# A two-block fp32 kernel on one core: moving the key decays' transfers, the W_in sums and the W_out negations

## The chip, the cores and the metric

The kernel runs on one core of a Trainium2 chip. The metric is the device time of one execution in microseconds (us). An execution that is profiled gives a page and a trace; "span" is the time from its first to its last instruction, and the execution's own time is a little longer. Engines: TensorE (PE; PEld are its weight loads), VectorE (DVE), ScalarE (ACT), GpSimd (POOL) and SyncE (SP), which only issues transfers.

## What is computed

A recurrent retention block (4 batches, 8 heads, 768 positions, head size 64) and then a two-layer block on its 3072 x 512 output, with 2048 hidden values:

```python
gamma = 1.0 - 2.0 ** (-5.0 - np.arange(H))
for t in range(S):
    state = gamma * state + einsum('bhd,bhe->bhde', k[:, :, t], v[:, :, t])
    y[:, :, t] = scale * einsum('bhd,bhde->bhe', q[:, :, t], state)
x = y.transpose(0, 2, 1, 3).reshape(B * S, H * D)
h = x @ w_in
sp = np.maximum(h, 0.0) + np.log1p(np.exp(-np.abs(h)))
g = h * erf(sp)
out = g @ w_out
```

All of it is float32 on the chip. W_in and W_out come as 64-bit words and are turned into fp32 on the chip.

## The kernel before

**Retention** is done in chunks of 128 positions, j = 0 to 23. The decays are put in by scaling keys and queries with a power of gamma for each position (`kq_s`), and later chunks (j of 6 and more) use a second layout in blocks of 32 positions, whose scales are `kq_b` and `by_b`. `load_block_scales` (L506) fills their first column from the constant key decays: 16 small transfers issued by GpSimd (L510, 0.5 KB each) and one for `by_b` (L514). `block_scales` (L516) makes the rest: three small DVE operations (L517 to L519), then five GpSimd products (L521). `prepared(j)` (L574) scales and transposes a chunk on DVE in five steps.

**The weights** are loaded in 14 pieces by SP (L281, L289) into parts of the weight tiles that are still unused, and converted by DVE and ACT (`whole_conversion`, L302, with L325 to L342; `shifted_conversion`, L349). The first piece of W_in is the first that a matmul needs.

**The two-layer block** works in groups. Groups g = 0 to 3 (the first 512 rows of x, `hidden` and `project`) each make 512 of the 2048 hidden values with plain matmuls (L895, L931). `hidden(g, u)` ends in an ACT copy into `HS[g]` (L913). Groups 4 to 23 (G0 = 4, NG = 24) come in pairs, one pair to a chunk of 256 rows; the even group of a pair uses the first half of the weights (s = 0), the odd one the second (s = 1). They use a fast matrix product: 26 products for the first layer and seven for the second, which need sums of blocks:

- `sum_in(s, upto)` (L381) makes the 30 sums of W_in's half s in place, in the order of the table `W_SUMS`: one DVE operation of 128x256 each (L385). It makes those not yet made, up to the number given.
- `sums(s)` (L388), run through `last_steps`, makes four blocks of W_out's half s: ACT copies a block negated (L393), then GpSimd issues a transfer of 512 KB within SBUF that adds another block to it (L394). The second block, T2, is made from the first, T1, and the fourth, T4, from T2; the third, T3, stands for itself.
- `x_sums(g)` (L956) makes sums of x, `hidden_steps(g)` (L977) the first layer. A step is a product of two weight blocks with one block of x into one of four PSUM banks (L986); the readings of that bank then follow, the first to write a part of h on ACT (L1000, L1002), the others adding to it on DVE (L998). A bank is written again by a later step once it has been read: step 9 writes the bank of step 5, step 15 that of step 13, step 25 that of step 24.
- After the first layer come the softplus (L858, ACT), a visit of the retention (`sub_visit`, L754, with the mask L676), the error function (L865, ACT), and `gated(g)` (L881), two DVE products of 128x1024 (L884). The second layer of group g - 1 (`project_part`, L1069) stands partly inside the first layer of group g, after steps 14, 18 and 24, and partly behind it.

**The order** is written by hand: every engine runs its instructions in the order in which the program names them, and waits on semaphores where it needs another engine's result. In the loop over the groups, tables named `order` say after which of the 26 steps a piece of other work (`next_chunk`, `e_sums`, `w_sums`, `last_steps`) is put in. For groups 0 to 3 the table `after` does this; `load_block_scales` stands there behind the last part of group 2's first layer. Nothing in its transfers waits for that place: GpSimd's queue issues them as soon as it comes to them. `put_first(tt)` (L942) copies a result of the first 512 rows on ACT (L944).

Of the kernel before, what the change touches and what calls it, by code (L numbers as in the profile page):

```python
# [48 lines left out]
W_SUMS = (  # L49
    (16, 2, 6, "+"),  # L50
    (17, 8, 10, "-"),
    (4, 4, 17, "+"),
    (10, 10, 16, "+"),
    (18, 16, 4, "-"),
    (19, 18, 5, "-"),
    (20, 1, 19, "-"),
    (20, 0, 20, "+"),
# [82 lines left out]
def kernel(  # L140
# [13 lines left out]
    nc = tc.nc  # L154
# [9 lines left out]
    N = FG * TCH  # L164
# [58 lines left out]
    idle_out = const.tile([P, 1], F32, name="idle_out")  # L223
# [8 lines left out]
    def w_out_of(ft):  # L232
        half, s, i = ft // (2 * FG), ft % (2 * FG) // FG, ft % FG
        return w_out_sb[:, s, 2 * half : 2 * half + 2, i, :]
# [144 lines left out]
    in_sums = [0, 0]  # L379

    def sum_in(s, upto):  # L381

        assert all(("hidden", 2 * FG + s * FG + u) in done for u in range(FG))
        for to, a, b, sign in W_SUMS[in_sums[s] : upto]:
            nc.vector.tensor_tensor(w_in_sb[:, s, to], w_in_sb[:, s, a], w_in_sb[:, s, b], op=OP[sign])  # L385
        in_sums[s] = max(in_sums[s], upto)
# [25 lines left out]
    def later_sums():  # L412
        for s in range(2):
            yield from sums(s)

    weight_steps = weights()
    last_steps = later_sums()
# [9 lines left out]
    def need(*what):  # L427
        nonlocal room
        while what not in done:
            cost = next(weight_steps, None)  # L430
            if cost is None:
                next(last_steps)
            room -= cost or 0
# [69 lines left out]
    kq_b = const.tile([P, NC, 2, HP, 4], F32, name="kq_b")  # L503
    by_b = const.tile([P, 2, HP], F32, name="by_b")

    def load_block_scales():  # L506
        for s, d in itertools.product(range(2), range(2)):
            part = slice((2 * s + d) * 32, (2 * s + d + 1) * 32)
            for u in range(HP):
                nc.gpsimd.dma_start(  # L510
                    kq_b[part, 0, 0, u],
                    decay_k[:, 2 * u + s : 2 * u + s + 1].rearrange("(a p) h -> p (a h)", p=32),
                )
        nc.gpsimd.dma_start(by_b[:, 1], decay_s)  # L514
# [25 lines left out]
    def ret_psum(pool=None):  # L540

        pool = pool or (next(psum_turn) if early else ps_r)
        return pool.tile([P, HP, C], F32, name="hp" if pool is ps_h else "r")
# [121 lines left out]
    def sub_scores(j):  # L665
        for hp in range(HP):
            for a, s in itertools.product(range(2), range(2)):
                t, own = slice(a * D, (a + 1) * D), slice(s * D, (s + 1) * D)
                nc.tensor.matmul(  # L669
                    SC[j][s][t, hp, :D], KT[j][own, hp, t], QT[j][own, hp, t], start=True, stop=True,  # L670
                )
# [11 lines left out]
    def sub_additions(j):  # L683

        for u in range(HP):
            for r in range(2):
                for a in adds_of[j]:
                    t, h = slice(a * D, (a + 1) * D), 2 * u + r
                    nc.tensor.matmul(
                        SC[j][a][r * D : (r + 1) * D, u, D:], KQ[j][t, 0, h, :], V[j][t, h, :],  # L690
                        start=True, stop=True,
                    )
        pace(1)
# [55 lines left out]
    def sub_begin(j, pool=None):  # L749
        SC[j] = [ret_psum(pool) for _ in range(2)]  # L750
        sub_scores(j)
        sub_additions(j)
# [98 lines left out]
    HS, E, O = {}, {}, {}  # L851

    def gate_softplus(g):


        name = "r" if g < 4 and g % 2 else "e"
        E[g] = act.tile([P, N], F32, name=name, bufs=1)
        nc.scalar.activation(E[g], HS[g], AF.Softplus)  # L858
# [10 lines left out]
    def pace_around(n):  # L869


        pace(n / 2)
        run(waiting)
        waiting.clear()
        pace(n / 2)
# [5 lines left out]
    def gated(g, part=None):  # L881
        for a in range(2) if part is None else (part,):
            half = slice(a * N // 2, (a + 1) * N // 2)
            nc.vector.tensor_tensor(E[g][:, half], HS[g][:, half], E[g][:, half], op=ALU.mult)  # L884
            pace(-1.1)
# [34 lines left out]
    def project(g, tt):  # L920
        if g == 0 and tt == 0:
            O[0] = [ps_o.tile([P, d_model], F32, name=f"o{i}") for i in range(TT)]
        step = tt
        if g:
            of = [(tt, u) for u in range(FG)]
        else:
            of = [(step % 2 * 2 + i // 2, step // 2 * 2 + i % 2) for i in range(4)]
        need("out", g * FG + max(u for _, u in of))
        for tt, u in of:
            ft = g * FG + u  # L930
            nc.tensor.matmul(  # L931
                O[0][tt].rearrange("p (d c) -> p d c", d=2),
                E[g][:, u * TCH + tt * P : u * TCH + (tt + 1) * P],
                w_out_of(ft),
                start=(ft == 0),
                stop=(ft == n_ft - 1),
            )
        if step == TT - 1:
            done.add(("project", g))
        pace_around(3.4)  # L940

    def put_first(tt):  # L942
        o = E[G0 - 1].rearrange("p (u t c) -> p t u c", u=FG, t=TT)[:, tt]
        nc.scalar.copy(o, O[0][tt].rearrange("p (u c) -> p u c", u=FG))  # L944
        nc.sync.dma_start(out[tt * P : (tt + 1) * P, :].rearrange("p (u c) -> p u c", u=FG), o)
# [7 lines left out]
    def chunk_of(g):  # L953
        return TCH // SCH + (g - G0) // 2
# [186 lines left out]
    def next_scores():  # L1141
# [31 lines left out]
            ([], []),  # L1173
            ([], []),
            ([(T, 5)], []),
            ([(load_block_scales,)], []),
        ],
        [
            ([(load, 6), (sub_results, 5)], []),
# [34 lines left out]
    def all_of(steps):  # L1214
        for _ in steps:
            pass
# [10 lines left out]
    load(j + 2)  # L1227
    gated(G0 - 1)
    next(last_steps)
    project(G0 - 1, 0)  # L1230
    put_first(0)
    sum_in(0, len(W_SUMS))
    next_chunk = prepared(j + 1)
    next(next_chunk)
    sub_begin(j)
    sub_states(j)
    next(last_steps)
    project(G0 - 1, 1)
    put_first(1)
    sum_in(1, 8)  # L1240
    order = {8: (last_steps,), 20: (next_chunk, last_steps)}
    order.update({n: (next_chunk,) for n in (10, 14, 16)})
    for n, _ in enumerate(hidden_steps(G0), start=1):
        for steps in order.get(n, ()):
            next(steps, None)
    all_of(next_chunk)
    nc.scalar.activation(idle, idle, AF.Softplus)
    gate_softplus(G0)
    sub_visit(j, G0)
    load(j + 3)  # L1250
    gate_erf(G0)
    sum_in(1, 20)
    for tt in range(2, TT):
        project(G0 - 1, tt)
        put_first(tt)
    gated(G0)
    sum_in(1, 24)
    j += 1

    def sums_left(s):  # L1260
        while in_sums[s] < len(W_SUMS):
            sum_in(s, in_sums[s] + 1)
            yield

    w_sums = sums_left(1)
    put = None
    for g in range(G0 + 1, NG):
        even = (g - G0) % 2 == 0
        more = j < NJ
        if put is not None:  # L1270
            put_part(put, 0)
        e_sums = g_sums(g - 1)
        next(e_sums)
        next_chunk = prepared(j + 1) if even or put is None else iter(())

        if put is not None:
            order = {18: (e_sums,), 20: (e_sums,), 24: (e_sums, e_sums)}
        else:
            order = {
                10: (next_chunk,), 14: (next_chunk, e_sums), 16: (next_chunk, e_sums),  # L1280
                18: (next_chunk, e_sums), 20: (e_sums,), 24: (next_chunk,),
            }
        if g == G0 + 1:
            order.update({n: (w_sums,) for n in (1, 2, 3, 4, 5, 6)})
            order.update({n: (last_steps,) for n in (11, 17, 23)})
        for n, _ in enumerate(hidden_steps(g), start=1):
            if put is not None and n in (14, 16, 18):
                put_part(put, n // 2 - 6)
            for steps in order.get(n, ()):
                next(steps, None)  # L1290
            if n in (14, 18, 24):
                project_part(g - 1, {14: 1, 18: 2, 24: 4}[n])
        put = None
        all_of(e_sums)
        all_of(next_chunk)

        nc.scalar.activation(idle, idle, AF.Softplus)
        gate_softplus(g)
        if more:
            sub_visit(j, g)  # L1300
        all_of(w_sums)
        if g == G0 + 1:
            all_of(last_steps)
        if g + 1 < NG and not even:
            x_sums(g + 1)
        if more:
            if even:
                all_of(prepared(j + 2))
            if j + 3 < NJ:
                load(j + 3)  # L1310
            j += 1
        gate_erf(g)
        for p in (5, 6, 7, 3):
            project_part(g - 1, p)
        if even:
            put = chunk_of(g - 1)
        if g == NG - 1:
            last_gated(g)
        else:
            gated(g)  # L1320

    g, m = NG - 1, chunk_of(NG - 1)
# [68 lines left out]
```

## Time and profile before

| | |
|---|---|
| median of 3 runs | 665.0 us (664.99 to 665.27) |
| the profiled execution, its own time | 664.47 us |
| its span | 662.8 us |
| PE busy in the span | 654.1 us (99%), 6240 instructions |
| DVE busy | 504.5 us (76%) |
| ACT busy | 289.6 us (44%) |
| GpSimd busy | 21.0 us (3%) |
| granted TensorE clock, mean | 1.000 |

The views used below: the page; the waits (for each engine and line, whom it waited for, with the sum, the number of times and the longest in us); the timeline (start in us from the beginning of the span, length in us, engine, line, operation, what it writes and reads, how many in a row, and in brackets the idle time of the engine before it and what ended it); and the windows (the busy time and number of instructions of each engine in a stretch, then granted clock, busy share of the 16 DMA engines and GB/s). Neighbouring matmul records overlap, since matmuls are pipelined.

### The profile page before, as it was taken

Reading aid. Unit: us, or ns where it says so; the run is one execution under the profiler, and the core shown is the slowest. Engines: PE = TensorE matmul, PEld = TensorE weight load, DVE = VectorE, ACT = ScalarE, POOL = GpSimd, SP = SyncE. Lnnn points to the kernel's source line nnn. Section 1 sums busy time; section 2 is a strip of 40 time slices with the busy share of each in tenths; the row PEclk is TensorE's granted clock in tenths of the full one; section 3 lists DMA queues with packets and bytes.
Section 4 is the critical chain, followed back from the end, with each engine's and each line's share of the span. In section 5 each row is a group of like instructions: output and inputs, shape, how many; then the busy total and the mean of one; then the engine's idle time right before and its main releaser. Section 6 shows DMA issues by size and latency. Waiting matters only on the chain.

```text
span 662.8 us, 15378 instructions
## 1 busy us (share of the span) xinstructions
PE 654.1 (99%) x6240; PEld 556.5 (84%) x6240; DVE 504.5 (76%) x1112; ACT 289.6 (44%) x410; POOL 21.0 (3%) x48
## 2 busy tenths in 40 slices
PE   8999999999999999999999999999999999999998
PEld 7744454476999999999999999999999999999997
DVE  5899989978886787778678678777787688476464
ACT  3368594445534344244244243442442542533440
POOL 7000001010200000000000000000000000000000
PEclk9999999999999999999999999999999999999999
DMA  9999973465842322222222322221231220000001
GB/s 181 218 251 199 227 252 57 73 129 106 159 78 55 75 36 49 65 47 47 71 42 46 75 38 49 46 65 33 48 79 35 43 57 1 1 35 1 0 33 33
DMA packets 157512, 51.90 MB, mean 78 GB/s; under 512 B 141313, under 2 KB 147841, under 8 KB 157441
## 3 DMA queue, kind: packets, MB, share of 16 engines
q1 hardware_dynamic: 155328, 46.71, 33.1%
q0 software_dynamic: 1696, 4.21, 3.5%
q8 instruction: 49, 0.80, 0.5%
q14 instruction: 23, 0.18, 0.1%
q10 hardware_dynamic: 416, 0.01, 0.0%
HBM read 40.39 MB, written 6.29 MB: 70 GB/s over the span
## 4 chain that ended last, share of the span: by engine, by line
PE 76%; DVE 8%; SPq 7%; DMA 4%; ACT 3%; issue 2%; ACTq 0%; DVEq 0%
PE o L1069 37%; PE hp L986 22%; PE r L986 11%; SPq L190 5%; DMA w_in_sb<-in_moe_w_in_dram 2%; PE r L777 2%; SPq L212 1%; DVE xs L336 1%; PE hp L669 1%; DVE w_in_sb L385 1%; DMA w_out_sb<-in_moe_w_in_dram 1%; PE o L813 1%; DVE w_in_sb L333 1%; DVE xs L325 1%; DMA kq<-in_k_dram 1%
## 5 line engine op out<-in xcount | busy, mean ns | idle before, releaser
L986 PE MATMUL hp<-xs,w_in_sb 128*128 128x128 f32 x1040 | 145.7, 275 | 2.3 <-DVE h L998 2.3
L1069 PE MATMUL o<-w_out_sb,h 128*128 128x256 f32 (+1 forms) x640 | 142.7, 381 | 0.0
L986 PEld LDWEIGHTS hp<-xs,w_in_sb 128*128 128x128 f32 x1040 | 134.9, 192 | 5.8 <-DVE h L998 2.9
L998 DVE TENSOR_TENSOR h<-h,hp 128x256 f32<-128x256 f32 x200 | 82.2, 419 | 74.9 <-PE hp L986 69.8
L1069 PEld LDWEIGHTS o<-w_out_sb,h 128*128 128x128 f32 x640 | 119.5, 190 | 16.6
L1069 PE MATMUL o<-w_out_sb,e 128*128 128x256 f32 x480 | 113.5, 379 | 0.0
L858 ACT ACTIVATE e<-h 128x2048 f32<-128x2048 f32 x22 | 42.0, 1911 | 123.8 <-DVE h L998 123.7
L1069 PEld LDWEIGHTS o<-w_out_sb,e 128*128 128x128 f32 x480 | 86.9, 190 | 9.4
L998 DVE TENSOR_TENSOR h<-h,r 128x256 f32<-128x256 f32 x160 | 59.9, 415 | 22.1 <-PE r L986 21.0
L1000 ACT COPY h<-hp 128x256 f32<-128x256 f32 x40 | 14.9, 372 | 134.1 <-PE hp L986 122.0
L986 PE MATMUL r<-xs,w_in_sb 128*128 128x128 f32 x480 | 66.7, 275 | 0.0
L986 PEld LDWEIGHTS r<-xs,w_in_sb 128*128 128x128 f32 x480 | 60.0, 192 | 0.0
L895 PE MATMUL hp<-xT,w_in_sb 128*128 128x512 f32 (+2 forms) x144 | 56.8, 548 | 0.6 <-DVE w_in_sb L342 0.6
L884 DVE TENSOR_TENSOR e<-h,e 128x1024 f32<-128x1024 f32 x42 | 49.3, 1213 | 8.0 <-ACT e L865 8.0
L895 PEld LDWEIGHTS hp<-xT,w_in_sb 128*128 128x128 f32 x144 | 25.6, 190 | 28.1 <-issue 24.6
L986 PE MATMUL hp<-xT,w_in_sb 128*128 128x128 f32 x320 | 48.8, 275 | 0.0
L986 PEld LDWEIGHTS hp<-xT,w_in_sb 128*128 128x128 f32 x320 | 43.7, 192 | 1.9 <-issue 1.0
L865 ACT ACTIVATE e<-e 128x2048 f32<-128x2048 f32 (+1 forms) x23 | 42.1, 1836 | 0.2
L1002 ACT ACTIVATE h<-hp 128x256 f32<-128x256 f32 x60 | 23.0, 383 | 31.5 <-PE hp L986 30.1
L986 PE MATMUL r<-xT,w_in_sb 128*128 128x128 f32 x240 | 33.3, 275 | 0.0
L865 ACT ACT_TABLE_LOAD x24 | 30.8, 1283 | 0.4
L986 PEld LDWEIGHTS r<-xT,w_in_sb 128*128 128x128 f32 x240 | 30.0, 192 | 0.0
(175 smaller groups left out, 777.0 us busy)
## 6 DMA issues: line engine op xcount, KB each, us to landing
w_out_sb<-in_moe_w_out_dram SPq DMA_DIRECT2D x14, 512.0 KB, 7.9
kq<-in_k_dram SPq DMA_DIRECT2D x23, 256.0 KB, 3.9
v<-in_v_dram SPq DMA_DIRECT2D x23, 256.0 KB, 3.4
out_dram<-r SPq DMA_DIRECT2D x23, 256.0 KB, 2.3
kq<-in_q_dram SPq DMA_DIRECT2D x288, 16.0 KB, 1.8
kb<-in_k_dram SPq DMA_DIRECT2D x288, 16.0 KB, 1.7
w_in_sb<-in_moe_w_in_dram SPq DMA_DIRECT2D x8, 512.0 KB, 12.5
w_out_sb<-w_out_sb POOLq DMA_DIRECT2D x8, 512.0 KB, 5.1
```

The lines of the kernel that those rows point to most:

```text
L190: nc.sync.dma_start(to[part, u * C : (u + 1) * C].rearrange("p (a d) -> p a d", d=32), src[2 * u + s, :, d * 32 : (d + 1) * 32].rearrange( ...
L212: nc.sync.dma_start(KQ[j][:, i], src[b, :, now, :].rearrange("h p d -> p h d"))
L777: nc.tensor.matmul(pp[r][col * D : (col + 1) * D, u % 2, t], x[own, u, :], QT[j][own, u, t], start=first(r, col), stop=True, skip_group_ch ...
L858: nc.scalar.activation(E[g], HS[g], AF.Softplus)
L865: nc.scalar.activation(E[g][:, half], E[g][:, half], AF.Erf)
L884: nc.vector.tensor_tensor(E[g][:, half], HS[g][:, half], E[g][:, half], op=ALU.mult)
L895: nc.tensor.matmul(HP_[ft][:, t], w_in_of(ft, kk), XC[0][:, kk, t], start=(kk == 0), stop=(kk == n_k - 1),)
L986: nc.tensor.matmul(to[:, u, :], w_in_sb[:, s, w, u * P : (u + 1) * P], XS[m](x), start=first and u == 0, stop=True, skip_group_check=True,)
L998: nc.vector.tensor_tensor(h, h, of, op=ALU.add if plus else ALU.subtract)
L1000: nc.scalar.copy(h, of)
L1002: nc.scalar.activation(h, of, AF.Copy, scale=-1.0)
L1069: nc.tensor.matmul(O[m][i][:, half, at], G[g][a][:, u * P : (u + 1) * P], w_out_sb[:, s, OUT[b], u, at], start=i not in started, stop=(s = ...
```

## The change

1. `load_block_scales` takes a group number and first has GpSimd copy the last column of that group's hidden values into a scratch tile. The 17 transfers stand behind this copy in GpSimd's queue, and it is called for group 2.
2. The 30 sums of W_in's second half were made 8 before group 4's first layer, 12 behind its visit, 4 behind its gating, and 6 inside group 5's first layer. Now 2 are made ahead of the scores of chunk 6 (`sub_begin`), 11 before group 4's first layer, 3 behind that layer, and 14 behind its visit and ahead of its gating.
3. Of the four steps that make W_out's first-half sums, the second goes ahead of the first projection of group 3, the third comes where the second was, and the fourth comes behind group 4's error function. They were the second behind the first projection, the third and the fourth inside group 4's first layer (after steps 8 and 20). Those of the second half stay where they were.

```diff
--- before.py
+++ after.py
@@ -503,7 +503,8 @@
     kq_b = const.tile([P, NC, 2, HP, 4], F32, name="kq_b")
     by_b = const.tile([P, 2, HP], F32, name="by_b")
 
-    def load_block_scales():
+    def load_block_scales(g):
+        nc.gpsimd.tensor_copy(idle_out, HS[g][:, N - 1 :])
         for s, d in itertools.product(range(2), range(2)):
             part = slice((2 * s + d) * 32, (2 * s + d + 1) * 32)
             for u in range(HP):
@@ -1173,7 +1174,7 @@
             ([], []),
             ([], []),
             ([(T, 5)], []),
-            ([(load_block_scales,)], []),
+            ([(load_block_scales, 2)], []),
         ],
         [
             ([(load, 6), (sub_results, 5)], []),
@@ -1227,42 +1228,38 @@
     load(j + 2)
     gated(G0 - 1)
     next(last_steps)
+    next(last_steps)
     project(G0 - 1, 0)
     put_first(0)
     sum_in(0, len(W_SUMS))
     next_chunk = prepared(j + 1)
     next(next_chunk)
+    sum_in(1, 2)
     sub_begin(j)
     sub_states(j)
     next(last_steps)
     project(G0 - 1, 1)
     put_first(1)
-    sum_in(1, 8)
-    order = {8: (last_steps,), 20: (next_chunk, last_steps)}
-    order.update({n: (next_chunk,) for n in (10, 14, 16)})
+    sum_in(1, 13)
+    order = {n: (next_chunk,) for n in (10, 14, 16, 20)}
     for n, _ in enumerate(hidden_steps(G0), start=1):
         for steps in order.get(n, ()):
             next(steps, None)
     all_of(next_chunk)
+    sum_in(1, 16)
     nc.scalar.activation(idle, idle, AF.Softplus)
     gate_softplus(G0)
     sub_visit(j, G0)
     load(j + 3)
     gate_erf(G0)
-    sum_in(1, 20)
+    next(last_steps)
+    sum_in(1, len(W_SUMS))
     for tt in range(2, TT):
         project(G0 - 1, tt)
         put_first(tt)
     gated(G0)
-    sum_in(1, 24)
     j += 1
 
-    def sums_left(s):
-        while in_sums[s] < len(W_SUMS):
-            sum_in(s, in_sums[s] + 1)
-            yield
-
-    w_sums = sums_left(1)
     put = None
     for g in range(G0 + 1, NG):
         even = (g - G0) % 2 == 0
@@ -1281,7 +1278,6 @@
                 18: (next_chunk, e_sums), 20: (e_sums,), 24: (next_chunk,),
             }
         if g == G0 + 1:
-            order.update({n: (w_sums,) for n in (1, 2, 3, 4, 5, 6)})
             order.update({n: (last_steps,) for n in (11, 17, 23)})
         for n, _ in enumerate(hidden_steps(g), start=1):
             if put is not None and n in (14, 16, 18):
@@ -1298,7 +1294,6 @@
         gate_softplus(g)
         if more:
             sub_visit(j, g)
-        all_of(w_sums)
         if g == G0 + 1:
             all_of(last_steps)
         if g + 1 < NG and not even:
```

## The prediction

> **What bounds the kernel now.** I read the page first, then TensorE's waits, then its timeline around each wait, and last the other engines at those places.
>
> ```profile
> span 662.8 us, 15378 instructions
> PE 654.1 (99%) x6240; PEld 556.5 (84%) x6240; DVE 504.5 (76%) x1112; ACT 289.6 (44%) x410; POOL 21.0 (3%) x48
> ```
>
> TensorE (PE) is busy for all but 8.7 us of its span, at the full granted clock. The change touches no matmul, so all that it can win lies in those 8.7 us. The view of waits says whom PE waited for (us in total, times, longest):
>
> ```profile
> PE hp L986 <- DVE h L998: 2.3, 3, 1.0
> PE o L536 <- POOL ident masks.py:199: 1.5, 1, 1.5
> PE hp L895 <- DVE w_in_sb L342: 0.6, 1, 0.6
> ```
>
> The rest is the last output (PE ends near 659.8) and scraps of 0.2 to 0.3 us before 15 us. L536 is the very first work and untouched. So two rows matter: L895, one wait, and L986, three waits. The timeline of PE places them (start, length, operation, and in brackets the idle time before it):
>
> ```profile
> 22.11 0.27 PE L598 MATMUL hp<-qT,kT 64*128 64x128 f32 x1
> 22.97 3.13 PE L895 MATMUL hp<-xT,w_in_sb 128*128 128x384 f32 x8 [0.58 <-DVE w_in_sb L342]
> ...
> 143.79 0.71 PE L986 MATMUL hp<-xs,w_in_sb 128*128 128x128 f32 x4 [0.78 <-DVE h L998]
> ...
> 149.04 0.71 PE L986 MATMUL hp<-xs,w_in_sb 128*128 128x128 f32 x4 [0.51 <-DVE h L998]
> ...
> 162.00 0.61 PE L986 MATMUL r<-xT,w_in_sb 128*128 128x128 f32 x4
> 163.61 1.16 PE L986 MATMUL hp<-xs,w_in_sb 128*128 128x128 f32 x8 [1.00 <-DVE h L998]
> ```
>
> Between 23 and 143 us and after 164 us PE never waits before the tail, so a microsecond won at one of these four places should arrive at the end.
>
> **Part 1: the key decays move.** Before, GpSimd issues the 17 small transfers as soon as it is free, from 6.38 to 16.82:
>
> ```profile
> 6.38 5.75 POOL L510 DMA_DIRECT2D kq_b<-decay_k_dram  x10
> ```
>
> They land 4 to 6.6 us after issue, so they run from about 9 to 22 us, exactly while the first chunks and the first piece of W_in come in. The windows view shows what the core's DMA engines moved (last two columns: busy share, GB/s):
>
> ```profile
> 7.00:9.00 2.00, 1.68 (x21) 1.32 (x22) 1.41 (x3) 1.17 (x2) 2.00 (x5) 1.00 1.35 219
> 11.00:13.00 2.00, 2.00 (x32) 1.71 (x30) 1.47 (x3) 0.52 (x1) 1.64 (x4) 1.00 1.36 192
> 13.00:15.00 2.00, 1.66 (x36) 1.35 (x36) 1.39 (x4) 1.15 (x4) 1.62 (x3) 1.00 1.36 188
> 17.00:19.00 2.00, 2.00 (x36) 1.75 (x32) 1.90 (x4) 0.90 (x3) 0.00 (x0) 1.00 1.19 184
> ```
>
> The engines are full in all four; the rate falls from 219 to 192, 188 and 184 GB/s when the small packets come. And VectorE (DVE), which turns the first piece into fp32, sits idle for it:
>
> ```profile
> 21.05 0.29 DVE L325 TENSOR_SCALAR xs<-w_out_sb 128x256 uint32<-128x256 uint32 x1 [2.13 <-DMA w_out_sb<-in_moe_w_in_dram]
> ```
>
> How much earlier would the piece land? Lower end: only the time that the small packets themselves are booked for is given back. In the DMA view of 9 to 20 us they have 4.9% of the engines' time, 0.54 us. Upper end: all 11.96 us from 9.0 to 20.96 run at 219 instead of 194 GB/s (mean of the six such windows): 11.96 x (1 - 194/219) = 1.4 us. I take about 1.2 us, nearer to the rates, because a fall in rate is what other transfers feel. PE can use only its own wait: 0.58 us of idle, plus 0.07 us because PE's next operation normally starts about 0.07 us before the record ahead of it ends (L638 starts at 26.02, L895 ends at 26.10). So the first row gives **0.65 us**, 0.54 at the lower end. The DVE work behind the piece (L325 to L342, five operations a slice) shifts by the same or more, so PE does not run into it one matmul later.
>
> What the move adds: one copy of a column on GpSimd (the 64x64 copies of L467 take 0.23 us) that waits for ScalarE's last copy of the third group's hidden values. That copy (L913) starts at 86.47 and takes 0.56 us, so the wait ends at 87.1. Behind it on GpSimd stand the 17 issues, then the five small products L521 at 110.5, and nothing else until 123. The issues took 10.4 us, so they end near 97.8; with the longest landing seen, 6.6 us, all is there by 104.4. DVE's first reader is L517 at 109.92: 5.5 us of slack, covered by DVE's conversions and gating of 87 to 110 us. In the new place the transfers meet the last pieces of the weights, in windows with a DMA share of 1.02 (80 to 90) and 0.54 (90 to 100); the same 0.54 to 1.4 us of delay there is behind conversions whose results PE needs at 114.7 and later. ScalarE waits 0.78 us for such a piece at 84.20, but that is before the copy releases anything. Cost: nothing.
>
> **Part 2: the sums of W_in's second half.** Thirty sums of 128x256 are made on DVE (L385, 420 ns each; in a row they start 0.37 to 0.41 us apart). Before, 8 stand ahead of group 4's first layer, 12 behind its visit, then the gating L884, then 4, then 6 inside group 5's first layer. DVE's timeline at the third L986 wait:
>
> ```profile
> 157.82 2.35 DVE L884 TENSOR_TENSOR e<-h,e 128x1024 f32<-128x1024 f32 x2
> 160.09 3.13 DVE L385 TENSOR_TENSOR w_in_sb<-w_in_sb 128x256 f32<-128x256 f32 x8
> 163.14 0.41 DVE L998 TENSOR_TENSOR h<-h,hp 128x256 f32<-128x256 f32 x1
> 163.47 0.88 DVE L385 TENSOR_TENSOR w_in_sb<-w_in_sb 128x256 f32<-128x256 f32 x2
> ```
>
> Here is the cause: step 5's reading (L998) stands behind eight sums, and step 9 writes the same bank. A step takes 0.45 us (158.87 to 159.32), so step 9 was due at 162.00 + 0.45 = 162.45 and came at 163.61: **1.16 us** lost. In group 6, without sums, step 9 follows 3.57 us after the first step, which is 162.44 here.
>
> After the change: two sums (0.8 us) go into DVE's idle 1.06 us before the mask L676 at 133.17: free. Eleven instead of eight follow at 134.17 and end at 134.17 + 11 x 0.41 = 138.7, ahead of the first reading at 139.10, which waits for PE: free, margin 0.4. Three (1.2 us) go ahead of the next mask, where DVE idled 1.14 us: 0.1 at most, and no matmul waits for that mask. Fourteen remain, from 153.42 to 153.42 + 14 x 0.385 = 158.8; gating ends at 161.1; step 5's result is there at 158.87 + 2.50 = 161.37 (group 6: 186.06 to 188.56). DVE is in time by 0.3 us, and PE would feel it only 0.7 us later still. So the whole 1.16 us goes.
>
> **Part 3: the negations of W_out's first half** (L393 on ScalarE, 1.05 us; each is followed by a 512 KB adding transfer from GpSimd, L394, 0.87 us to issue, 4.7 to 7.8 to land). The second moves ahead of a projection: it waits for the first one's landing (123.20 + 5.1 = 128.3) and ends near 129.4; the copy queued behind it (L944) ran at 132.13. Free. The third goes from 140.19 to about 132.7, into an idle stretch of 3.1 us. Free. The fourth goes from 145.26 to behind the error function, 156.4, and pushes L944 there by about 1.06 us; its next copy waits for PE until 159.07 anyway. Its transfer is issued near 157.7, past no other GpSimd work, and lands by 165.5; its reader, the last projection inside group 5's first layer, is at 174.31. What leaves the first layer is ScalarE time at 140.19, ahead of a copy at 141.26 that DVE does not wait for (DVE is in a row from 140.97). So the 0.78 us at 143.79, set by a key scaling (L587) and six readings in a row, stays; so does the 0.51 us at 149.04, where two steps in succession use one bank with nothing between. Gain: 0; at the outside both go, 1.29.
>
> **Sum.** 664.47 (the profiled execution: 662.8 of span, 1.7 around it) - 0.65 - 1.16 = 662.66. The median of the runs is 0.53 above the profiled one, so **663.2 us**, 0.27% less than 665.0. About 0.2%, 1.33 us, is what a measurement of this kernel can tell from no change; it lies at 663.7.
>
> **Rivals.**
> *Only the sums count (663.9).* The 0.65 is lost again because DVE does not follow: the gating L884 before the fourth group's projection ends at 127.66, PE needs it at 128.45, a margin of 0.8 that shrinks to 0.15. Against it: DVE starts earlier too, and the first matmuls read only its first half.
> *Only the start counts (664.35).* The sums come out longer, or another wait takes the place of the 1.16. The margins are 0.3 and 0.7 us; group 6 shows that layer running without a stall.
> *Nothing arrives (665.0).* A transfer late in the run decides. PE's missing waits after 164 us speak against it.
> *Slower (675).* GpSimd now issues its transfers while DVE is 83 to 98% busy (windows of 90 to 110). If each issue had to wait for a DVE operation of 1.23 us, the longest kind there, 17 x (0.55 + 1.23) = 30.3 us from 87.1, plus 5.5 to land, is 122.9, 13 us after L517 wants it; PE's margin takes 0.8, so 663.2 + 12. It starts to matter when an issue takes over (109.9 - 87.1 - 5.5)/17 = 1.0 us. Against it: eight larger issues (L394) stand among busy DVE stretches at 123 to 182 us and took 0.87 to 0.93 us. The Trainium skill (SBUF — State Buffer, Who interferes with whom) states such a lock: a DVE operation in a two-port mode shuts GpSimd out of the port through which it writes descriptors. By its example (620 ns alone, 3100 ns beside a copy) the issues would take five times as long; no row here shows it.
>
> **How the numbers follow.** Both gains: 0.68, own range 662.8 to 663.6. Sums only 0.13, start only 0.08, nothing 0.05, slower 0.06. The range takes in the single gains, the lower end of the landing and half of the other two waits: 662.6 to 664.4. Faster by over 0.2% is the first case without its upper edge, 0.66; slower 0.06; within, 0.28.
>
> **What would show it.** Right: no wait of PE on L342 near 22 us, DVE's 2.13 us shorter, 215 GB/s and more in 11 to 15 us; no wait near 162 us, 143 and 149 still there; L510 from 87 to 98. Wrong: DVE idle at L517, a new PE wait on L884 near 128, or PE waits on L998 in group 5.

## The result, and the profile after

| | before | after |
|---|---|---|
| median, on one chip | 664.57 us (7 runs, 664.12 to 665.27) | 662.61 us (7 runs, 662.09 to 664.43) |
| ratio, with its 95% interval | | 0.9973 [0.9961, 0.9984] |
| the profiled execution, its own time | 664.47 us | 662.09 us |
| its span | 662.8 us | 660.4 us |

The change makes the kernel faster by 1.8 us by the ratio (0.0027 x 664.57) and by 1.96 us by the medians; forecast was 1.8 us. (The forecast time, 663.2 us, started from a median of 665.0 for the kernel before; beside the kernel after it took 664.57.) Single executions of several kernels (the one before, and e1, e8, e10 and e11 of the experiments) took 2.8 to 6.6 us more than the median of their kernel at a mean granted clock of 0.995 to 0.997; none of these is among the profiles, so the reason is open, and they shift the ratios and widen the intervals of the kernels that had one or two.

In everything that follows, lines of the kernel after the change carry numbers that are higher by one from L507 on: L986 has become L987, L998 L999, L895 L896, L884 L885, L510 L511, L517 L518. The page of the kernel after begins:

```profile
span 660.4 us, 15375 instructions
PE 653.7 (99%) x6240; PEld 556.7 (84%) x6240; DVE 504.9 (76%) x1112; ACT 289.9 (44%) x410; POOL 22.0 (3%) x49
```

The number of matmuls and of DVE instructions is the same, and so is their busy time within 0.4 us. Of the 2.4 us by which the span is shorter, 2.0 are idle time of PE (6.7 us instead of 8.7); the other 0.4 are busy time, and two records below show where. The view of waits of the kernel after, for PE, says which:

```profile
PE o L537 <- POOL ident masks.py:199: 1.5, 1, 1.5
PE hp L987 <- DVE h L999: 1.3, 2, 0.8
```

The row for L342 (0.6 us) is gone, and the row for L999 has two waits (1.3 us) instead of three (2.3 us). PE's timeline after, at the four places:

```profile
22.12 2.85 PE L896 MATMUL hp<-xT,w_in_sb 128*128 128x384 f32 x8
...
142.66 0.71 PE L987 MATMUL hp<-xs,w_in_sb 128*128 128x128 f32 x4 [0.79 <-DVE h L999]
...
147.91 0.71 PE L987 MATMUL hp<-xs,w_in_sb 128*128 128x128 f32 x4 [0.51 <-DVE h L999]
...
160.87 0.61 PE L987 MATMUL r<-xT,w_in_sb 128*128 128x128 f32 x4
161.32 1.06 PE L987 MATMUL hp<-xs,w_in_sb 128*128 128x128 f32 x8
```

The first and the last line have lost the bracket that stood behind them before, and both records are shorter: 2.85 instead of 3.13 us, and 1.06 instead of 1.16. The two waits in group 4 are as they were (0.78 and 0.51 before). On the way there the differences between the two spans can be read off by the same instruction in both: at the first transposes after 17 us 0.19 us, at the second group of W_in matmuls (28.11 before, 26.98 after) 1.13, at group 4's first layer (136.60 and 135.47) 1.13 still, at group 6's (186.06 and 183.67) 2.39, and 2.40 at the end. So the gain is made at two places, 1.13 in the start and 1.27 in group 5, and nothing is given back. Of the 1.13, the 0.19 had been gained before any of the small transfers was issued in the kernel before, at 6.38 (the first chunk's queries landed at 5.43 us, before the change at 5.65 us), so that part is chance.

DVE's timeline after, at the same places:

```profile
19.00 0.30 DVE L325 TENSOR_SCALAR xs<-w_out_sb 128x256 uint32<-128x256 uint32 x1 [0.27 <-DMA w_out_sb<-in_moe_w_in_dram]
...
108.10 0.17 DVE L518 RECIPROCAL by_b<-by_b 128x4 f32<-128x4 f32 x1
...
152.30 5.53 DVE L385 TENSOR_TENSOR w_in_sb<-w_in_sb 128x256 f32<-128x256 f32 x14
157.74 2.35 DVE L885 TENSOR_TENSOR e<-h,e 128x1024 f32<-128x1024 f32 x2
160.25 0.42 DVE L999 TENSOR_TENSOR h<-h,hp 128x256 f32<-128x256 f32 x1 [0.15 <-PE hp L987]
```

The first piece of W_in is there 2.05 us earlier (19.00 for 21.05), and DVE's idle time ahead of it is 0.27 us for 2.13. The key decays' first reader L518 waits for nothing at 108.10. And the reading L999 of group 5, which stood behind eight sums, now waits 0.15 us for PE, and PE not for it.

The windows of the kernel after (last two columns: busy share of the DMA engines, GB/s):

```profile
11.00:13.00 2.00, 2.00 (x32) 1.71 (x30) 1.46 (x4) 0.59 (x1) 0.00 (x0) 1.00 1.35 217
13.00:15.00 2.00, 1.66 (x39) 1.35 (x36) 1.39 (x3) 1.22 (x3) 0.00 (x0) 1.00 1.34 223
...
17.00:19.00 2.00, 2.00 (x36) 1.61 (x33) 1.71 (x5) 1.10 (x3) 0.00 (x0) 1.00 0.92 223
```

The fifth pair, GpSimd, is 0.00 there; it was 1.64 and 1.62 in the first two. The rate is 217 to 223 GB/s in the place of 192, 188 and 184. (The window left out, 15 to 17 us, has 203 GB/s at a busy share of 0.98, where before had 199 at 1.27: there the DMA engines have less to do.) GpSimd's own timeline has the issues in their new place:

```profile
85.63 9.18 POOL L511 DMA_DIRECT2D kq_b<-decay_k_dram  x16
94.80 0.58 POOL L515 DMA_DIRECT2D by_b<-decay_s_dram  x1
```

### The profile page after: what moved, and what is told of

Same layout as the page of the kernel before. It is cut to its first block, busy times and chain, and to the rows that moved or that the text cites. A ratio compares the mean times of both kernels' runs of the same rounds, so it can differ in the third digit from the quotient of the medians.

```text
span 660.4 us, 15375 instructions
## 1 busy us (share of the span) xinstructions
PE 653.7 (99%) x6240; PEld 556.7 (84%) x6240; DVE 504.9 (76%) x1112; ACT 289.9 (44%) x410; POOL 22.0 (3%) x49
## 4 chain that ended last, share of the span: by engine, by line
PE 98%; DMA 1%; DVE 1%; issue 0%; SPq 0%; ACT 0%; DVEq 0%
PE o L1070 37%; PE hp L987 23%; PE r L987 12%; PE o L932 8%; PE hp L896 8%; PE r L778 2%; PE hp L670 1%; PE o L814 1%; DMA kq<-in_k_dram 1%; PE r L599 1%; PE o L646 1%; PE r L793 1%; PE hp L793 1%; PE r L566 1%; DVE h L999 0%; PE r L814 0%
## 5 line engine op out<-in xcount | busy, mean ns | idle before, releaser
L987 PE MATMUL hp<-xs,w_in_sb 128*128 128x128 f32 x1040 | 145.6, 275 | 1.3 <-DVE h L999 1.3
L987 PEld LDWEIGHTS hp<-xs,w_in_sb 128*128 128x128 f32 x1040 | 135.0, 192 | 4.6 <-DVE h L999 1.7
L999 DVE TENSOR_TENSOR h<-h,hp 128x256 f32<-128x256 f32 x200 | 82.2, 420 | 73.8 <-PE hp L987 68.7
L999 DVE TENSOR_TENSOR h<-h,r 128x256 f32<-128x256 f32 x160 | 60.0, 416 | 23.0 <-PE r L987 21.9
L987 PE MATMUL r<-xs,w_in_sb 128*128 128x128 f32 x480 | 66.7, 275 | 0.0
L987 PEld LDWEIGHTS r<-xs,w_in_sb 128*128 128x128 f32 x480 | 60.0, 192 | 0.0
L896 PE MATMUL hp<-xT,w_in_sb 128*128 128x512 f32 (+2 forms) x144 | 56.5, 548 | 0.0
L885 DVE TENSOR_TENSOR e<-h,e 128x1024 f32<-128x1024 f32 x42 | 49.3, 1214 | 8.0 <-ACT e L866 8.0
L987 PE MATMUL hp<-xT,w_in_sb 128*128 128x128 f32 x320 | 48.7, 275 | 0.0
L896 PEld LDWEIGHTS hp<-xT,w_in_sb 128*128 128x128 f32 x144 | 25.7, 190 | 27.0 <-issue 24.6
L987 PEld LDWEIGHTS hp<-xT,w_in_sb 128*128 128x128 f32 x320 | 43.7, 192 | 1.9 <-issue 1.0
L987 PE MATMUL r<-xT,w_in_sb 128*128 128x128 f32 x240 | 33.3, 275 | 0.0
L987 PEld LDWEIGHTS r<-xT,w_in_sb 128*128 128x128 f32 x240 | 30.0, 192 | 0.0
```

Source lines behind the costliest of these rows:

```text
L896: nc.tensor.matmul(HP_[ft][:, t], w_in_of(ft, kk), XC[0][:, kk, t], start=(kk == 0), stop=(kk == n_k - 1),)
L987: nc.tensor.matmul(to[:, u, :], w_in_sb[:, s, w, u * P : (u + 1) * P], XS[m](x), start=first and u == 0, stop=True, skip_group_check=True,)
L999: nc.vector.tensor_tensor(h, h, of, op=ALU.add if plus else ALU.subtract)
```

## Experiments

The theory is that of the prediction: the start is won because the first piece of W_in lands earlier once the small packets are out of its way; group 5 is won because its first layer no longer stands behind eight sums; the negations win nothing, and the new place of the transfers costs nothing. Against it stand four rivals: the start's gain is lost again later (or was chance), the second gain comes from the negations, the new place costs something that the larger gains hide, and the two waits that stay in group 4 hide a gain that could still be had.

**Each part alone** (the kernel before, with one part of the change at a time; parts 1 and 2 were measured twice).

Part 1 alone, e1_keys and e10_keys, is the first two hunks of the diff:

```diff
-    def load_block_scales():
+    def load_block_scales(g):
+        nc.gpsimd.tensor_copy(idle_out, HS[g][:, N - 1 :])
...
-            ([(load_block_scales,)], []),
+            ([(load_block_scales, 2)], []),
```

> The kernel before with part 1 alone: the key decays wait on GpSimd for group 2's hidden values; sums and negations as before. My theory (the small packets slow the transfers ahead of the first piece of W_in): the first matmul on W_in no longer waits for DVE, DMA rate of 215 GB/s and more between 9 and 15 us, the start gains 0.65 to 1.1 us, the wait near 162 us stays at 1.0 us; time 0.65 to 1.1 below before. Rival (what the first matmul gained is chance from execution to execution, the packets are too small to matter): gain 0.2 or less, and the wait of 0.58 still there.

> The kernel before with the move of the key decays alone, a second time, for a narrower interval. Theory: 0.6 to 1.1 below the kernel before. Rival (chance of the start): 0.2 or less.

Part 2 alone, e2_sums and e11_sums:

```diff
+    sum_in(1, 2)
     sub_begin(j)
...
-    sum_in(1, 8)
+    sum_in(1, 13)
...
+    sum_in(1, 16)
     nc.scalar.activation(idle, idle, AF.Softplus)
...
-    sum_in(1, 20)
+    sum_in(1, len(W_SUMS))
...
-            order.update({n: (w_sums,) for n in (1, 2, 3, 4, 5, 6)})
```

> The kernel before with part 2 alone: all sums of W_in's second half stand ahead of group 4's gating; key decays and negations as before. My theory: the PE wait of 1.0 us in group 5 goes and nothing takes its place, gain 1.16 to 1.27; the wait for DVE's first piece near 22 us and the two waits in group 4 stay. Rival (part 1 is needed first, because DVE is otherwise late in 127 to 140 us): a new wait of PE on DVE between 128 and 140 us, gain under 0.8.

> The kernel before with the sums alone, a second time. Theory: 1.0 to 1.3 below the kernel before, and together with the decays alone as much as the whole change.

Part 3 alone, e3_negs:

```diff
     next(last_steps)
+    next(last_steps)
     project(G0 - 1, 0)
...
-    order = {8: (last_steps,), 20: (next_chunk, last_steps)}
-    order.update({n: (next_chunk,) for n in (10, 14, 16)})
+    order = {n: (next_chunk,) for n in (10, 14, 16, 20)}
...
     gate_erf(G0)
+    next(last_steps)
```

> The kernel before with part 3 alone: the negations of W_out's first half stand outside group 4's first layer. My theory: no gain, 0 within 0.3 us; all three waits of PE on DVE in the first layers (0.8, 0.5, 1.0) stay as they are. Rival (the negation at step 8 holds up ScalarE's reading at step 10 and so the wait at step 15): the wait of 0.8 shrinks and the time falls by up to 0.8.

The kernel after once more, e5_after, to have it beside the kernels that follow:

> The changed kernel once more, beside the others of this call. Theory: 1.8 to 2.4 below the kernel before (the start 0.65 to 1.1, group 5 1.17 to 1.27, negations 0). Rival (only the sums count over many executions): 1.2 below.

| kernel | median us (runs) | before, beside it | difference | ratio [95%] |
|---|---|---|---|---|
| e1_keys | 663.85 (11) | 664.61 | -0.76 | 0.9998 [0.9981, 1.0016] |
| e10_keys | 663.71 (12) | 664.56 | -0.85 | 0.9992 [0.9980, 1.0004] |
| e2_sums | 663.56 (11) | 664.61 | -1.05 | 0.9979 [0.9967, 0.9992] |
| e11_sums | 663.24 (12) | 664.56 | -1.32 | 0.9979 [0.9961, 0.9996] |
| e3_negs | 664.40 (11) | 664.61 | -0.21 | 0.9996 [0.9987, 1.0005] |
| e5_after | 662.34 (12) | 664.39 | -2.05 | 0.9963 [0.9946, 0.9979] |

The sums alone make the kernel faster, both times. The keys alone gave 0.76 and 0.85 us by the medians, but both intervals include 1: their gain rests on the profiles, not on these times. The negations alone are within what can be told from nothing. The parts add up: 0.8 + 1.2 + 0.2 = 2.2 beside 1.96 and 2.05 for the whole.

The profiles say where. In e1 the start is as in the kernel after (no row for L342 among PE's waits, the first L325 at 19.08, and at 19.14 in e10), and the wait in group 5 is still there, in PE's timeline of e1:

```profile
162.52 1.16 PE L987 MATMUL hp<-xs,w_in_sb 128*128 128x128 f32 x8 [1.00 <-DVE h L999]
```

In e2 it is the other way round: group 5 takes 25.92 us from its first matmul to group 6's, as in the kernel after, and PE's timeline of e2 still waits in the start (here the lines have before's numbers):

```profile
23.33 3.13 PE L895 MATMUL hp<-xT,w_in_sb 128*128 128x384 f32 x8 [0.85 <-DVE w_in_sb L342]
```

Group 5 takes 27.19 or 27.20 us in every profile without part 2 (before, e1, e3, e10) and 25.92 in every one with it (after, e2, e5, e6, e7, e9, e11), apart from e4 (27.45) and e8 (26.17) below, which change what stands in and ahead of that group. In e3 the waits of PE on L998 are before's:

```profile
PE hp L986 <- DVE h L998: 2.3, 3, 1.0
```

All three are there, the longest of 1.0 us too; so no part of the gain in group 5 belongs to the negations, and that rival falls.

**How much the start gives.** Since before's one profile may not be typical, the same two instructions are read in all profiles in which the transfers stand where they did before (before, e2, e3, e11) and in all in which none is issued early (after, e1, e4, e5, e6, e7, e8 and e10). DVE's first L325 starts at 21.05, 21.42, 20.66 and 20.48 in the first, 20.90 in the mean, and from 19.00 to 19.52, 19.26 in the mean, in the second: 1.64 us earlier. (In e4 and e10 DVE itself was later than the piece, so the landing gained a little more than that.) From 9 to 15 us the core moved 192 to 203 GB/s in the first four and 219 to 220 in the eight. PE gains less. From the fourth chunk's transposes to the second group of W_in matmuls it takes 10.13, 10.47, 9.29 and 9.56 us in the first and 9.19 to 9.20 in every one of the second: the gain is 0.10 to 1.28 us, 0.67 in the mean. It depends on how late PE itself comes: in e3 its transposes start at 18.42, 0.44 later than before's, and PE's waits have no row for L342; only its weight loads still wait for it.

To see whether the delay follows the number of packets, e9_half leaves half of them in the old place:

```diff
     def load_block_scales(g):
-        nc.gpsimd.tensor_copy(idle_out, HS[g][:, N - 1 :])
         for s, d in itertools.product(range(2), range(2)):
+            if (s, d) == (1, 0):
+                nc.gpsimd.tensor_copy(idle_out, HS[g][:, N - 1 :])
```

> The changed kernel with 8 of the 16 key-decay transfers at the start again, as in the kernel before, and the other 8 behind the copy. Theory (each small packet takes time from the transfers that run beside it, so the delay goes by their number): the first piece of W_in lands about halfway, 19.9 to 20.3 us for its second transfer instead of 20.6 to 21.3 with all and 18.9 to 19.4 with none; that is just in time for PE, so the time is that of the changed kernel within 0.4. Rival (any small packets at the start do it, through one late DMA engine): it lands at 20.6 or later and the time is 0.6 or more above the changed kernel.

It took 662.63 us (7 runs; ratio 0.9970 [0.9959, 0.9981]), as the kernel after. Its first piece lands late all the same, in DVE's timeline of e9:

```profile
20.49 0.29 DVE L325 TENSOR_SCALAR xs<-w_out_sb 128x256 uint32<-128x256 uint32 x1 [1.43 <-DMA w_out_sb<-in_moe_w_in_dram]
```

20.49 is as late as in e11 (20.48) with all sixteen in the old place, and behind the 19.9 to 20.3 of the theory, so a cost proportional to the number of packets is not shown; the rival's price, 0.6 us or more, did not come either. The core moved 196 GB/s from 9 to 15 us, near the 192 of before, and 234 from 15 to 17, where its second half was missing. PE's stretch was 9.43 us, 0.23 more than without any, and inside the spread of those with all. One profile can't say more.

**Does the new place cost anything?** e7_none puts a memset on GpSimd in the place of the sixteen transfers of the key decays:

```diff
         nc.gpsimd.tensor_copy(idle_out, HS[g][:, N - 1 :])
-        for s, d in itertools.product(range(2), range(2)):
...
+        nc.gpsimd.memset(kq_b[:, 0, 0], 1.0)
         nc.gpsimd.dma_start(by_b[:, 1], decay_s)
```

> The changed kernel without the 16 transfers of the key decays; a constant stands in their place, so the decays of the later chunks are left out of the result. Theory: in their new place the transfers cost nothing, so the time is that of the changed kernel within 0.3. Rival (they still slow the last pieces of the weights, which come in at the same time): 0.3 to 1.0 below it.

It took 662.66 us (12 runs), 0.3 more than e5_after's 662.34 beside it. Taking the sixteen transfers out wins nothing: as far as such medians can tell, their new place is free, and the rival that it costs 0.3 us or more falls.

**The slower rival, made to happen.** e6_late lets the copy wait for the end of a tile of group 3 in place of one of group 2, so that the seventeen issues come some 20 us later:

```diff
-        nc.gpsimd.tensor_copy(idle_out, HS[g][:, N - 1 :])
+        nc.gpsimd.tensor_copy(idle_out, HS[g][:, TCH - 1 : TCH])
...
-            ([(load_block_scales, 2)], []),
+            ([], []),
...
-            ([(load, 6), (sub_results, 5)], []),
+            ([(load_block_scales, 3), (load, 6), (sub_results, 5)], []),
```

> The changed kernel with the key decays' transfers released one layer later, by the first part of group 3's hidden values (near 102.6 us instead of 85.7). Theory: the issues take 9.7 us and land 2 to 4 us later, at 114.5 to 116, so that DVE, which wants them at 108.1, waits 6.4 to 7.9 us at the first reciprocal; DVE's gating for the fourth group then ends 5 to 6.5 us after PE wants it, and the time rises by 5 to 6.5 against the changed kernel. Rival (the slack is larger than that, as DVE could catch up in later layers): under 3.

It took 670.21 us (7 runs; ratio to before 1.0082 [1.0057, 1.0107]), 7.9 us more than e5_after, which is above the 5 to 6.5 expected. The copy was released at 104.99 (ACT's L914 had stood behind conversions); the last of the sixteen landed at 115.70 and `by_b`, the one that L518 reads, at 116.43. Two lines carry the price, from DVE's and PE's timelines of e6, and a third, of e5, shows PE's line without it:

```profile
116.45 0.18 DVE L518 RECIPROCAL by_b<-by_b 128x4 f32<-128x4 f32 x1 [5.08 <-DMA by_b<-decay_s_dram]
...
133.36 5.30 PE L932 MATMUL o<-w_out_sb,r 128*128 128x512 f32 x8 [4.41 <-DVE r L885]
...
127.37 3.60 PE L932 MATMUL o<-w_out_sb,r 128*128 128x512 f32 x8
```

DVE idles 5.08 us for the landing, and L518 comes 8.35 us after the 108.10 of the kernel after (3.27 of this DVE was late by itself in that execution, where ScalarE had waited 2.90 us for a piece of the weights). The margins between DVE and PE take the rest, and PE waits 4.41 us for the gating. In e5 that projection starts at 127.37, here at 133.36: 5.99 us later, 0.31 of them brought from the start. But group 4 starts 7.69 us later (143.21 for 135.52). The other 1.70 stand in the length of the record, 5.30 for 3.60 us, and in the windows of e6, where the granted clock is the number behind the five pairs:

```profile
132.00:134.00 2.00, 0.64 (x1) 0.50 (x2) 2.00 (x3) 0.00 (x0) 0.00 (x0) 0.80 1.00 188
134.00:136.00 2.00, 2.00 (x3) 0.67 (x2) 1.97 (x6) 0.00 (x0) 0.00 (x0) 0.50 0.65 133
136.00:138.00 2.00, 2.00 (x5) 0.91 (x4) 1.90 (x6) 0.00 (x0) 0.00 (x0) 0.84 1.02 189
```

What the three windows lack of the full clock, 0.40, 1.00 and 0.32 us, is 1.72 us: after the wait PE works at half its clock (0.50) for about 3.4 us, twice that, and is at 1.00 again from 138 on. The Trainium skill (TensorE: Matmul & The Clock Gate, Part 1: The HAM clock gate (the "warmup" mystery)) says that an idle window of about 3.4 us halves the clock until PE has been busy for as long; this trace agrees, with 4.41 us of idle ahead of it and the 3.4 us behind it. The waits of up to 1.26 us in the other profiles left the clock at 1.00.

**Can the two waits that stay be had?** e4_fill takes the kernel after, puts half of a projection behind step 14 and half behind step 24 of group 4's first layer, and deals the sums out around them (`project_some` issues the matmuls of the parts that it is given):

```diff
-    sum_in(1, 13)
+    sum_in(1, 14)
...
+    part_of = {14: (0, 1), 24: (2, 3)}
+    sums_by = {5: 16, 16: 18, 24: 22}
...
+        if n in sums_by:
+            sum_in(1, sums_by[n])
+        project_some(2, part_of.get(n, ()))
...
-    sum_in(1, 16)
+    sum_in(1, 25)
...
-    for tt in range(2, TT):
-        project(G0 - 1, tt)
-        put_first(tt)
+    put_first(2)
+    project(G0 - 1, 3)
+    put_first(3)
```

> The changed kernel, with the matmuls of the projection of rows 256 to 383 of group 3 split in two halves and put behind steps 14 and 24 of group 4's first layer, where PE still waits for DVE (0.79 and 0.51), and the sums spread over DVE's gaps (14 ahead of the layer, 2 behind step 5, 2 behind step 16, 4 behind step 24, 3 behind step 26, 5 behind the visit). My theory: PE's two waits are DVE's reading of a bank, other matmuls cover them, gain 1.3 to 1.5 against the changed kernel, 3.1 to 3.8 against the kernel before. Rival (the cover that the projection gave behind the visit is then missing): the error function and the gating come late for group 5, a new wait of PE there of 0.5 to 3 us eats the gain or more.

It took 661.97 us (5 runs; ratio 0.9960 [0.9948, 0.9973]), 2.64 less than the kernel before beside it, where the theory asked for 3.1 to 3.8. Both waits of group 4 are gone, but a new one took their place, in PE's timeline of e4:

```profile
159.69 0.71 PE L987 MATMUL hp<-xs,w_in_sb 128*128 128x128 f32 x4 [1.26 <-ACT h L1001]
```

It is ACT that comes late. Its timeline of e4, behind the error function:

```profile
157.36 1.04 ACT L393 ACTIVATE w_out_sb<-w_out_sb 128x1024 f32<-128x1024 f32 x1
158.31 1.05 ACT L945 COPY r<-o 128x512 f32<-128x512 f32 x2
159.25 0.38 ACT L1001 COPY h<-hp 128x256 f32<-128x256 f32 x1
```

The first is the fourth negation, then come the two copies, and only then the first reading of group 5's first layer. In the kernel after, ACT waited 1.24 us between the two copies for PE's last projection, and the negation cost nothing there; e4 has moved one of the two projections into group 4, and that idle time is gone. By the starts, the negation holds the reading up by 0.95 us and the two copies by 0.94, so no more than 0.95 of the 1.26 us is the price of part 3 here, and either alone would have left a wait of some 0.3 us (estimates from these rows: no run moves one of them alone). e8_fill2 takes e4, moves this negation back to step 20 of group 4, spreads the copies, and puts the second half of the gating into group 5:

```diff
-    order = {n: (next_chunk,) for n in (10, 14, 16, 20)}
+    order = {n: (next_chunk,) for n in (10, 14, 16)}
+    order[20] = (next_chunk, last_steps)
...
+    put_first(2)
     sum_in(1, 25)
...
     gate_erf(G0)
-    next(last_steps)
...
-    put_first(2)
     project(G0 - 1, 3)
-    put_first(3)
-    gated(G0)
+    gated(G0, 0)
...
+            if (g, n) == (G0 + 1, 5):
+                gated(G0, 1)
+            if (g, n) == (G0 + 1, 7):
+                put_first(3)
```

> The kernel with the split projection in group 4's first layer, with ScalarE's queue cleared behind the error function: the fourth negation back behind step 20, the copy of the third projection ahead of the softplus, the copy of the fourth behind step 7 of group 5, and the second half of the gating behind step 5. Theory: the 1.26 us that PE waited for ScalarE's first reading in group 5 go to 0.3 or less, and the time is 1.0 to 1.4 below the changed kernel. Rival (DVE has no room for the gating inside group 5's first layer): a new wait of PE on DVE there of 0.5 to 1.0.

It took 660.94 us (12 runs; ratio to before 0.9954 [0.9931, 0.9978]), 1.40 us less than e5_after beside it, by the medians. The waits of PE in e8, from the longest on:

```profile
PE o L537 <- POOL ident masks.py:199: 1.5, 1, 1.5
PE o L639 <- DVE state L848: 0.3, 1, 0.3
```

No first layer waits any more. This version beats both kernels by the medians; that it beats the kernel after rests on one pair of medians (ten of its twelve executions are below the fastest of e5's twelve) and on its profile (span 658.9 for 660.4), as the intervals of the two ratios overlap.

## Why the prediction was right, point by point

**The bound.** It was put into PE's 8.7 us of idle time, at four waits, and the reasoning that a microsecond won there arrives at the end held: 1.13 of difference at 27 us is still 1.13 at 135, and 2.39 at 184 is 2.40 at the end. That all there is to win lies in the 8.7 us was not quite so: 0.28 us at the start and 0.10 in group 5 came out of records that count as busy.

**The start, 0.65 us.** The profiles give 0.67 in the mean, and 0.10 to 1.28 in single ones. So the size is right as a mean, but that is in part luck: the single losses are 0.93 (before), 1.28, 0.10 and 0.37, and the profile from which 0.65 was read had lost 0.93. The forecast hid that the term varies from execution to execution, which neither of its bounds (0.54 and 0.65) said. The profiled pair shows 0.94 (1.13 less the 0.19 of chance). That is 0.3 more than forecast because the wait was read as the bracket and 0.07 us of overlap alone. PE was held up inside the group of matmuls too, where the row was 3.13 us and is now 2.85. PE's own waits don't show it, but those of its weight loads do, in the view of waits of before:

```profile
PEld hp L895 <- DVE w_in_sb L342: 1.0, 2, 0.7
```

The second of the two stands at 24.54, ahead of the weights of the fifth matmul, with 0.66 us of idle time: the L342 of the piece's second half ended at 24.48. The prediction said that PE would not run into DVE one matmul later; before the change it did so four matmuls later. The two waits of the weight loads are there in e2, e3, e9 and e11 too (0.8 to 1.0 us), and in none of the profiles with all transfers in the new place. The landing came 1.64 us earlier in the mean, above the forecast's 1.2 and its upper end of 1.4. It was undersized, and that cost the forecast nothing, because PE could use no more than its own waits.

**The new place, nothing.** Right: e7 without the transfers is no faster. Their seventeen issues took 9.75 us (85.63 to 95.38; forecast 10.4), the last, `by_b`, landed at 99.9, and its reader came at 108.10, so 8.2 us of slack in the place of 5.5.

**The sums, 1.16 us.** Measured 1.27 (27.19 less 25.92 in group 5). The 1.16 that the prediction had worked out went as a whole; the other 0.10 is in the two steps behind the wait, which took 1.16 us after it and take 1.06 without one. The covers held with little to spare: the eleven sums ended at 137.43, which is 138.56 on before's clock (forecast 138.7), and the reading behind them waited 0.56 us for PE (forecast 0.4); the fourteen took 5.53 us (forecast 5.38), and DVE was at L999 0.15 us ahead of PE (forecast 0.3).

**The negations, nothing.** Right in this kernel (e3), and the waits at 143 and 149 us stayed at 0.79 and 0.51 as said. The prediction gave the reason for the fourth: ACT's next copy waits for PE anyway (1.24 us of idle time in the kernel after). It holds only while that projection stands where it does; e4 moved it, and there the negation is part of the 1.26 us that PE waits for ACT.

**The rivals.** "Only the sums count" rested on the gating L885 running late; no wait for it appears in the kernel after. "Only the start counts" falls by e2 and e11, "nothing arrives" by the result. The slower one asked for issues of 1.0 us and more: the sixteen took 548 to 781 ns, median 550 (548, 548 and 772 before), beside a DVE that was busy for 2.90 of the 3 us from 85 to 88 and from 88 to 91. A small part of such a delay is there: the two issues behind the first in which a whole TENSOR_SCALAR of DVE (L370, 0.43 us) ran, at 89.13 and 94.12, took 678 and 691 ns, and in e1, e4, e5, e8 and e10 the same two took 576 to 683, where the others behind the first two took 548 to 556. For a lock between DVE and GpSimd the Trainium skill (SBUF — State Buffer, Who interferes with whom) names `tensor_scalar` among the operations that can take the shared port; if this is that lock, it costs at most 0.14 us an issue here, and beside DVE's other operations nothing is seen. The rival's price was tested by e6: transfers that come too late do reach PE. L518 is 8.33 us later than in e5 and the projection 5.99, so the margin took 2.34 us, where the prediction's 12 let it take 0.8; the halved clock, for which the 12 had no term, then added 1.70.

**The sum.** 1.81 us forecast; 1.8 by the ratio, 1.96 and 2.05 by the medians of two measurements, 2.38 in the profiled pair. The pair exceeds the forecast by 0.19 of chance, 0.29 in the start and 0.11 in group 5.

## What to carry to other kernels

Where one engine is busy for 99% of the span, list its few waits, and price an edit by the wait that it takes away: what a transfer lands earlier (1.64 us) is not what the engine gains (0.67). When a wait goes, look at the length of the record behind it as well, and read the same wait in several executions before giving it one number. And an edit that costs nothing is hidden by something: the fourth negation was free because ScalarE would have waited for a projection, and once that was moved, it stood in the way of the reading that PE waited for.

## What the runs showed of the hardware that was not expected

- A wait of 4.41 us halved TensorE's granted clock for the next microseconds, and the eight matmuls behind it took 5.30 us for 3.60: 1.7 us on top of the wait. Waits of up to 1.26 us had no such effect.
- Small packets took more than the time they are booked for: 3.9% of the DMA engines' time from 9 to 15 us in the kernel before, but the rate there was 192 to 203 GB/s in the four profiles with them and 219 to 220 in the eight without, 7 to 12% less.
- Two steps of the first layer took 1.16 us behind a wait and 1.06 in a row, and one step 0.71 for 0.61. The 0.10 us are in the first matmul: its record is 377 ns long in place of 275. Why is open.
- Behind the first two of a row (772 to 783 and 589 to 592 ns), GpSimd's issue of one of the sixteen transfers took 548 to 556 ns, and 576 to 691 ns when one of DVE's TENSOR_SCALAR operations of 0.43 us ran wholly inside it.
